# Four K matmuls held back behind the last modulation columns, and two quarters' modulation begun with 128 tokens

## Chip, cores, metric

One core of one Trainium2 chip. The metric is the device time of one execution in microseconds (us); lower is better. The verdict "faster" or "slower" needs 2%; what this study looks at is about 0.1%, so most of the evidence comes from profiles, in which times can be compared to a hundredth of a microsecond, and only the rest from the timed runs.

Names: PE is the tensor engine, PEld its weight loads, DVE the vector engine, ACT the scalar engine, POOL GpSimd, SP the engine that issues most transfers. PSUM is the memory that PE writes its results to, used by the kernel in eight banks. The span is the time from the first to the last instruction of a run. A transfer's slack is the time from its landing to the start of the instruction that needs it. L680 is line 680 of the kernel.

## The reference, cut to what matters

```python
x = A_x                                             # 1 x 2048 x 1024, bf16
mod = (silu(c) @ w_mod).reshape(1, 6, 1, -1)        # 6 x 1024 values
sa, ca, ga, sb, cb, gb = ...                        # its six rows
h = layernorm(x) * (1 + ca) + sa                    # <- the stretch studied here
x = x + ga * linear_attention(h, wqkv, wo)          # q, k, v = h @ wqkv; phi(k)^T v; ...
h = layernorm(x) * (1 + cb) + sb
x = x + gb * ((gelu(h @ w_gate) * (h @ w_up)) @ w_down)
```

The first matmuls on real data need `h`, and `h` needs `ca` and `sa`, which are themselves a matrix product of `silu(c)` with 4 MB of `w_mod`. The beginning of the kernel is therefore a pipeline of arrivals: x, `w_mod` in four quarters of 256 features each, and the K weights.

## The kernel before

Tokens come in chunks of 128; the first four chunks (0 to 3) share one tile of 512 tokens. The 1024 features are cut into eight slices `dc` of 128; quarter q of the modulation serves slices 2q and 2q+1. The parts that the change and the argument touch:

```python
def mods(Ht, rfn, sg, sc, s0, s1, dc0, dc1, tag):          # DVE: h = h * (1+ca) + sa, one slice at a time
    for dc in range(dc0, dc1):
        e.tensor_scalar(Ht[sg][:, dc, s0:s1], Ht[sg][:, dc, s0:s1], sA, sB, op0=mult, op1=add)
def mod1(c0, n, dc0, dc1): ...                              # the same, for n chunks from chunk c0

def mod_cols(q, bank):                                      # PE: 32 matmuls of one column each
    for t in range(2):                                      # t: ca or sa, each its own transfer of 512 KB
        for b in range(2):
            for dc in range(NDC):
                e.matmul(PS(bank, col, col + 1), WMQ[q][:, dc, t, b*P:(b+1)*P], SILUT[:, dc:dc+1], ...)
def mod_copy(q, bank): ...                                  # DVE: PSUM columns -> MODT, with the 1 of (1+ca)

# K of chunks 0 to 3: eight PSUM tiles of 128 tokens x 512 features, seven whole banks ...
kb0 = {(0,0): 0, (0,1): 1, (1,0): 2, (1,1): 3, (2,0): 5, (2,1): 6, (3,0): 7}
def k31(dcs, c0=0, c1=496): ...                             # ... and chunk 3's second half, 496 wide, in bank 4,
                                                            # whose last 16 columns hold the modulation columns
def k_part(q, cs):
    for dc in (2*q, 2*q + 1):
        for (c_, jg), b in kb0.items():
            if c_ in cs: kv_mm(c_, "k", jg, b, [dc])
        if 3 in cs: k31([dc])

# [...]
        k_part(0, [3])
        k_part(1, [3])
        mod_cols(2, 4)                 # third quarter's columns
        mod_copy(2, 4)
        warm(2)                        # two matmuls of zeros, no result
        mod1(0, 4, 4, 6)               # slices 4 and 5, all 512 tokens
        k_part(2, [0, 1, 2, 3])        # 16 K matmuls
        mod_cols(3, 4)                 # last quarter's columns
        mod_copy(3, 4)
        mod1(0, 4, 6, 8)               # slices 6 and 7
        for (c_, jg), b in kb0.items():
            kv_mm(c_, "k", jg, b, [6, 7])
        k31([6, 7])
        k31(list(range(NDC)), MC0, 512)   # the 16 columns left over
# [...] K is evacuated, then V, then everything else
```

## Time and profile before

| | before |
|---|---|
| time, median of 3 runs | 839.61 us (838.99 to 839.78) |
| span of the profiled execution | 836.77 us |
| first modulation columns start | 9.20 us |
| third quarter's columns start | 21.06 us |
| first V matmul starts | 31.57 us |

The page of the profile: span, busy time of the engines, and the chain of work that ended last.

```profile
span 836.8 us, 11359 instructions
...
PE 830.2 (99%) x4194; PEld 384.4 (46%) x4194; DVE 511.7 (61%) x895; ACT 336.1 (40%) x555; POOL 37.1 (4%) x91
...
PE 98%; DMA 1%; DVE 1%; SPq 0%; ACT 0%; issue 0%
```

PE is busy from end to end and the chain is 98% PE: the time is PE's stream of instructions plus its gaps. Which gaps there are is told by PE's waits in the whole run (engine, tile and line; what it waited for; us in total, times, longest).

```profile
PE ps_all L478 <- POOL bmask L429: 2.1, 1, 2.1
PE ps_all L680 <- DVE h1T L565: 1.3, 4, 0.7
PE ps_all L602 <- DMA wmq<-in_w_mod_dram: 0.6, 1, 0.6
```

Three lines, all in the first 30 us. The second is the one that the change is after: K matmuls (L680) that wait for the modulated h1T. They are seen in order of time in PE's timeline (start, us, engine, line, operation, what it writes and reads, shapes, count, and in brackets the idle time before it):

```profile
9.20 0.95 PE L602 MATMUL ps_all<-siluT,wmq 128*128 128x1 bf16 x32 [0.59 <-DMA wmq<-in_w_mod_dram]
...
21.06 0.94 PE L602 MATMUL ps_all<-siluT,wmq 128*128 128x1 bf16 x32
21.86 0.59 PE L736 MATMUL ps_all<-warm 128*128 128x512 bf16 x2
22.71 1.69 PE L680 MATMUL ps_all<-wk,h1T 128*128 128x512 bf16 x7 [0.25 <-DVE h1T L565]
24.23 0.37 PE L756 MATMUL ps_all<-wk,h1T 128*128 128x496 bf16 x1
24.44 1.67 PE L680 MATMUL ps_all<-wk,h1T 128*128 128x512 bf16 x7
25.95 0.37 PE L756 MATMUL ps_all<-wk,h1T 128*128 128x496 bf16 x1
26.16 0.94 PE L602 MATMUL ps_all<-siluT,wmq 128*128 128x1 bf16 x32
27.81 3.30 PE L680 MATMUL ps_all<-wk,h1T 128*128 128x512 bf16 x14 [0.71 <-DVE h1T L565]
30.95 0.77 PE L756 MATMUL ps_all<-wk,h1T 128*128 128x496 bf16 x10
31.57 0.81 PE L680 MATMUL ps_all<-wv,h1T 128*128 128x512 bf16 x3
```

And DVE's timeline of the same stretch:

```profile
22.04 0.16 DVE L611 TENSOR_TENSOR modt<-ps_all,add 128x4 f32<-128x4 f32 x1 [3.41 <-PE ps_all L602]
22.24 0.74 DVE L565 TENSOR_SCALAR h1T<-h1T,modt 128x512 bf16<-128x512 bf16 x2
27.14 0.16 DVE L611 TENSOR_TENSOR modt<-ps_all,add 128x4 f32<-128x4 f32 x1 [4.16 <-PE ps_all L602]
27.34 0.73 DVE L565 TENSOR_SCALAR h1T<-h1T,modt 128x512 bf16<-128x512 bf16 x2
```

The hand-over: last column matmul, copy by DVE, modulation of one slice by DVE, PE again. The 32nd column matmul starts at 26.94 and the next K matmul at 27.81, 0.87 us later. The same hand-over at 22 us is partly covered by the two matmuls of zeros (0.25 us of idle time before PE's restart instead of 0.71).

### The profile page before, as it was taken

The page shows a single profiled execution, that of the slowest core. Times are in us where ns is not written, and L with a number is a line of the kernel's source. Part 1 is how long each engine was busy: PE and PEld are TensorE (multiplying, and loading weights), DVE is VectorE, ACT ScalarE, POOL GpSimd, SP SyncE. Part 2 cuts the span into 40 slices and gives each one's busy share as a digit, 9 for nine tenths or more (in the row PEclk, how much of TensorE's full clock was granted, in tenths as well). Part 3 has the DMA queues.
Part 4 walks back from the last instruction along what each step waited for, and adds up shares of the span by engine and source line. Part 5 has one row for each costly group of instructions (what it writes and reads, how often), then busy time and mean ns, then how long its engine had stood idle before and what let it go on. Part 6 is the DMA issues. An engine that isn't in the chain of part 4 may idle for free.

```text
span 836.8 us, 11359 instructions
## 1 busy us (share of the span) xinstructions
PE 830.2 (99%) x4194; PEld 384.4 (46%) x4194; DVE 511.7 (61%) x895; ACT 336.1 (40%) x555; POOL 37.1 (4%) x91
## 2 busy tenths in 40 slices
PE   8999999999999999999999999999999999999998
PEld 4444444444444444444444444444444444444445
DVE  6678877687785577753455665356556535655512
ACT  2357777446423355420354442045554104445300
POOL 2012111000200000010000000000000000000000
DMA  9984422239696769180555533055553305555000
GB/s 291 312 251 101 102 76 76 78 79 235 140 236 204 224 202 277 28 194 26 158 151 151 152 101 76 19 158 152 151 151 101 76 20 159 152 154 145 7 19 26
DMA packets 184102, 113.22 MB, mean 135 GB/s; under 512 B 35560, under 2 KB 175080, under 8 KB 183024
## 3 DMA queue, kind: packets, MB, share of 16 engines
q1 hardware_dynamic: 184032, 112.50, 50.0%
q8 instruction: 33, 0.54, 0.3%
q14 instruction: 21, 0.17, 0.1%
q10 hardware_dynamic: 16, 0.00, 0.0%
HBM read 100.67 MB, written 4.47 MB: 126 GB/s over the span
## 4 chain that ended last, share of the span: by engine, by line
PE 98%; DMA 1%; DVE 1%; SPq 0%; ACT 0%; issue 0%
PE ps_all L1144 23%; PE ps_all L1116 23%; PE ps_all L1119 23%; PE ps_all L680 13%; PE ps_all L1059 7%; PE ps_all L721 7%; PE ps_all L702 1%; DMA wmq<-in_w_mod_dram 1%; PE ps_all L961 0%; PE ps_all L602 0%; DVE h1T L565 0%; PE ps_all L973 0%; PE ps_all L756 0%; PE ps_all L643 0%; SPq L442 0%; DVE st L742 0%
## 5 line engine op out<-in xcount | busy, mean ns | idle before, releaser
L1116 PE MATMUL ps_all<-h2T,wg 128*128 128x512 bf16 x896 | 339.6, 379 | 0.0
L1119 PE MATMUL ps_all<-h2T,wu 128*128 128x512 bf16 x896 | 339.6, 379 | 0.0
L1144 PE MATMUL ps_all<-wd,yT 128*128 128x512 bf16 (+3 forms) x952 | 194.2, 366 | 0.0
L1127 ACT ACTIVATE q<-ps_all 128x512 f32<-128x512 f32 x112 | 66.9, 597 | 225.3 <-PE ps_all L1116 221.5
L1144 PEld LDWEIGHTS ps_all<-wd,yT 128*128 128x128 bf16 x952 | 90.1, 98 | 103.9 <-issue 0.4
L1116 PEld LDWEIGHTS ps_all<-h2T,wg 128*128 128x128 bf16 x896 | 87.7, 98 | 105.8 <-issue 0.2
L1119 PEld LDWEIGHTS ps_all<-h2T,wu 128*128 128x128 bf16 x896 | 87.7, 98 | 105.7
L1132 DVE SCALAR_TENSOR_TENSOR ww<-th,guh 128x512 f32<-128x512 f32 x112 | 77.5, 692 | 77.9 <-ACT th L1131 77.9
L1129 DVE SCALAR_TENSOR_TENSOR ww<-q,ps_all 128x512 f32<-128x512 f32 x112 | 76.9, 686 | 77.7 <-ACT guh L1128 77.6
L1131 ACT ACTIVATE th<-ww 128x512 f32<-128x512 f32 x112 | 70.5, 629 | 87.3 <-DVE ww L1129 87.3
L1149 DVE TENSOR_TENSOR ps_all<-ps_all,gbb 128x512 f32<-128x512 f32 (+3 forms) x34 | 22.7, 667 | 94.8 <-PE ps_all L1144 94.8
L1134 DVE TENSOR_TENSOR yT<-ww,ps_all 128x512 bf16<-128x512 f32 x112 | 76.8, 686 | 3.8
L1128 ACT ACTIVATE guh<-ps_all 128x512 f32<-128x512 f32 x112 | 66.3, 592 | 0.0
L721 PE MATMUL ps_all<-h1T,wq 128*128 128x512 bf16 x256 | 58.7, 379 | 0.0
L680 PE MATMUL ps_all<-wk,h1T 128*128 128x512 bf16 x248 | 57.3, 379 | 1.3 <-DVE h1T L565 1.3
L669 ACT ACTIVATE eb<-ps_all 128x512 f32<-128x512 f32 x64 | 37.4, 600 | 50.6 <-PE ps_all L680 22.3
L680 PE MATMUL ps_all<-wv,h1T 128*128 128x512 bf16 x256 | 57.7, 379 | 0.0
L1059 PE MATMUL ps_all<-w,pq 128*128 128x512 bf16 x256 | 56.2, 379 | 0.0
L670 DVE TENSOR_SCALAR eb<-eb 128x512 f32<-128x512 f32 x64 | 27.1, 423 | 26.7 <-ACT eb L669 26.3
L1059 PEld LDWEIGHTS ps_all<-w,pq 128*128 128x128 bf16 x256 | 25.0, 98 | 30.2 <-issue 0.2
L680 PEld LDWEIGHTS ps_all<-wv,h1T 128*128 128x128 bf16 x256 | 24.9, 98 | 29.5
L680 PEld LDWEIGHTS ps_all<-wk,h1T 128*128 128x128 bf16 x248 | 23.8, 98 | 30.6 <-DVE h1T L565 3.1
(96 smaller groups left out, 481.0 us busy)
## 6 DMA issues: line engine op xcount, KB each, us to landing
wg<-in_B_w_gate_dram SPq DMA_DIRECT2D x56, 512.0 KB, 4.1
wu<-in_B_w_up_dram SPq DMA_DIRECT2D x56, 512.0 KB, 5.3
rb<-scr_rd SPq DMA_DIRECT2D x32, 256.0 KB, 6.6
wd<-in_B_w_down_dram SPq DMA_DIRECT2D x7, 1024.0 KB, 8.5
wmst<-in_w_mod_dram SPq DMA_DIRECT2D x6, 1024.0 KB, 6.8
wmq<-in_w_mod_dram SPq DMA_DIRECT2D x8, 512.0 KB, 7.7
out_dram<-xall SPq DMA_DIRECT2D x31, 128.0 KB, 1.7
xall<-in_A_x_dram SPq DMA_DIRECT2D x3, 1024.0 KB, 12.4
```

Of the source, the lines that this page charges most:

```text
L680: o = sch.op(T, lambda e, dc=dc: e.matmul(PS(bank), H1[sg][:, dc, ci * P:(ci + 1) * P], W_[:, dc, jg * 512:(jg + 1) * 512], start=(dc == 0 ...
L721: o = sch.op(T, lambda e, dc=dc: e.matmul(PS(b), WQ[:, dc, qc * P:(qc + 1) * P], H1[sg][:, dc, :], start=(dc == 0), stop=(dc == NDC - 1)), ...
L1059: last[half] = sch.op(T, lambda e, g=g, half=half: e.matmul(PS(b0 + half), PQ[sg][:, g, ci * P:(ci + 1) * P], W2[:, g, half * 512:(half + ...
L1116: og = sch.op(T, lambda e, dc=dc: e.matmul(PS(bg), WG[slot][:, dc, e_ * P:(e_ + 1) * P], H2[sg][:, dc, :], start=(dc == 0), stop=(dc == ND ...
L1119: ou = sch.op(T, lambda e, dc=dc: e.matmul(PS(bu), WU[slot][:, dc, e_ * P:(e_ + 1) * P], H2[sg][:, dc, :], start=(dc == 0), stop=(dc == ND ...
L1127: sch.op(A, lambda e: e.activation(Q1[j][:, :], PS(bg), ACTF.Square, scale=math.sqrt(GELU_A)), prd=pr(bg), wr=rq, note=f"q1 {fc}")
L1128: ogh = sch.op(A, lambda e: e.activation(GUH[j][:, :], PS(bg), ACTF.Copy, scale=0.5), prd=pr(bg), wr=rg, note=f"gh {fc}")
L1129: sch.op(V, lambda e: e.scalar_tensor_tensor(WW[j][:, :], Q1[j][:, :], 1.0, PS(bg), op0=ALU.add, op1=ALU.mult), rd=rq, prd=pr(bg), wr=rw, ...
L1131: sch.op(A, lambda e: e.activation(TH[j][:, :], WW[j][:, :], ACTF.Tanh, scale=GELU_C), rd=rw, wr=rt, note=f"th {fc}")
L1132: sch.op(V, lambda e: e.scalar_tensor_tensor(WW[j][:, :], TH[j][:, :], 1.0, GUH[j][:, :], op0=ALU.add, op1=ALU.mult), rd=rt + rg, wr=rw, n ...
L1134: sch.op(V, lambda e: e.tensor_tensor(YT[:, fc, :], WW[j][:, :], PS(bu), ALU.mult), rd=rw, prd=pr(bu), wr=r_yt(fc), note=f"yT {fc}")
L1144: o = sch.op(T, lambda e, b=b, fc=fc, c0=c0, c1=c1, n=n: e.matmul(PS(b, 0, n), YT[:, fc, ci * P:(ci + 1) * P], WDT[fc // 4][:, fc % 4, c0:c1],
```

## The change

The intent: fill the gap behind the last columns with K matmuls that need only slices already modulated, and shorten the hand-over by modulating the first 128 tokens of a slice, all that the first two matmuls need, in an instruction of their own.

```diff
         warm(2)
-        mod1(0, 4, 4, 6)
-        k_part(2, [0, 1, 2, 3])
+        mod1(0, 1, 4, 5)
+        mod1(1, 3, 4, 5)
+        mod1(0, 4, 5, 6)
+        k_part(2, [0, 1, 2])
         mod_cols(3, 4)
         mod_copy(3, 4)
-        mod1(0, 4, 6, 8)
+        mod1(0, 1, 6, 8)
+        mod1(1, 3, 6, 8)
+        for dc in (4, 5):
+            kv_mm(3, "k", 0, kb0[3, 0], [dc])
         for (c_, jg), b in kb0.items():
             kv_mm(c_, "k", jg, b, [6, 7])
-        k31([6, 7])
+        k31([4, 5, 6, 7])
```

The change was announced as six matmuls held back. The diff holds back four (chunk 3, two halves, slices 4 and 5): two go into the gap, and the two 496-wide ones go to the end of the block. Of the four modulations, three are split (slices 4, 6 and 7); slice 5 stays 512 wide.

## The prediction

> **What bounds the kernel.** The tensor engine (PE): 830.2 of 836.8 us busy (page part 1), the chain of waits is 98% PE. The wait list has three entries for PE in the whole run: 2.1 us at the start, 0.6 us for a w_mod transfer, 1.3 us in four waits for the modulated h1T. The change touches two or three of those four, all before 32 us.
>
> **The stretch, from the timeline.**
> - Third quarter: modulation columns copied at 22.04; the 128x512 modulation of slice 4 takes 0.412 us from 22.238; PE restarts at 22.71. 16 K matmuls follow, one per 0.216 us, to 26.16. [...]
> - Last columns: 32 one-column matmuls, 26.16 to 26.96. Copy at 27.14, slice 6 modulated from 27.338 (0.413 us), PE restarts at 27.81: 0.85 us without a PE start. The next matmul waits for slice 7 until 28.13, 0.10 us over the pitch.
>
> **What the change does.** No matmul is added or removed. By the diff I count four held back (chunk 3, both halves, slices 4 and 5), not six: two go into the gap behind the last columns, two to the end of the K block. Four modulations of 128x512 become four of 128x128 (0.306 us) and four of 128x384 (0.377 us).
>
> **Costs on the critical path.**
> 1. First modulation 128 wide: PE restarts 0.106 us earlier, near 22.60. The other 384 tokens are ready near 22.90; the third matmul starts at 23.05, so no new stall.
> 2. 12, not 16, matmuls before the columns: they begin near 25.20, end near 26.0. Their last wmq transfer landed at 25.31 by its semaphore and is needed near 25.4. This uses up almost all of the DMA's slack.
> 3. The gap: two matmuls (0.43 us) fill it. Copy near 26.18, slice 6 for the first 128 tokens ready near 26.74; PE still idles about 0.3 us.
> 4. Slice 7's 0.10 us stall disappears; the last wk slice landed at 26.59, needed near 26.97.
> 5. Two matmuls (0.42 us) follow at the end.
>
> Sum: 0.43 filled + 0.106 + 0.107 + 0.10 = about 0.74 us. The K block ends near 30.62, not 31.36. VectorE's evacuation begins about 1 us earlier, wv's first half landed at 28.95 and 30.35 (needed near 30.8 and 31.7), and PE has no wait afterwards: nothing should absorb the shift.
>
> **Prediction.** 838.9 us, 8 in 10 between 838.0 and 839.9, where the runs before spread from 838.99 to 839.78. Faster by over 2%: 0.003; within 2%: 0.994; slower by over 2%: 0.003.
>
> **What would show the steps.** PE's restart at 22.60; columns starting at 25.2 without a wait for wmq; two matmuls in the gap and 0.3 us idle; the first V matmul near 30.8, not 31.57; PE's waits on h1T falling from 1.3 to about 0.6 us; past 50 us the same pieces of the chain, all 0.7 us earlier.
>
> **What would make it wrong.** The last wmq transfer landing late: in this trace one of its 16 parts trails the others by about 1.4 us, and every delay past 25.4 now costs PE time one for one, where before there was 0.9 us of slack. The same for wk's last slice. Or a later transfer (x, wq, FFN weights) that takes the gain back, which I don't expect, as PE waits for none today.

## The result, and the profile after

The change is correct. Its median was 838.83 us (838.45 to 839.15, 6 runs), that of the kernel before 839.3 us (838.66 to 839.78, 6 runs). The ratio is 0.9994, 95% interval 0.9981 to 1.0007: same, by the 2% rule. The times alone can't tell 0.5 us from nothing.

The page of the profile after:

```profile
span 836.7 us, 11362 instructions
...
PE 830.1 (99%) x4194; PEld 384.4 (46%) x4194; DVE 512.2 (61%) x898; ACT 336.4 (40%) x555; POOL 37.4 (4%) x91
```

The spans differ by 0.03 us (836.77 and 836.74). A reader who stops here concludes that the change did nothing. PE's waits in the whole run say otherwise:

```profile
PE ps_all L478 <- DMA c<-in_c_dram: 2.4, 1, 2.4
PE ps_all L602 <- DMA wmq<-in_w_mod_dram: 1.1, 1, 1.1
PE ps_all L680 <- DVE h1T L565: 0.7, 4, 0.2
```

The wait for h1T fell from 1.3 to 0.7 us as intended, and the wait of the first columns for their transfer rose from 0.6 to 1.1 us. The change doesn't touch that transfer. PE's timeline:

```profile
9.85 0.95 PE L602 MATMUL ps_all<-siluT,wmq 128*128 128x1 bf16 x32 [1.08 <-DMA wmq<-in_w_mod_dram]
...
21.75 0.94 PE L602 MATMUL ps_all<-siluT,wmq 128*128 128x1 bf16 x32
22.55 0.59 PE L736 MATMUL ps_all<-warm 128*128 128x512 bf16 x2
23.30 2.76 PE L680 MATMUL ps_all<-wk,h1T 128*128 128x512 bf16 x12 [0.15 <-DVE h1T L565]
25.90 0.94 PE L602 MATMUL ps_all<-siluT,wmq 128*128 128x1 bf16 x32
26.70 0.59 PE L680 MATMUL ps_all<-wk,h1T 128*128 128x512 bf16 x2
27.45 3.20 PE L680 MATMUL ps_all<-wk,h1T 128*128 128x512 bf16 x14 [0.15 <-DVE h1T L565]
30.49 1.18 PE L756 MATMUL ps_all<-wk,h1T 128*128 128x496 bf16 x12
31.53 0.81 PE L680 MATMUL ps_all<-wv,h1T 128*128 128x512 bf16 x3
```

DVE's timeline of the same stretch (a row merges instructions of one line and shows the shape of the first):

```profile
22.73 0.16 DVE L611 TENSOR_TENSOR modt<-ps_all,add 128x4 f32<-128x4 f32 x1 [3.41 <-PE ps_all L602]
22.93 0.93 DVE L565 TENSOR_SCALAR h1T<-h1T,modt 128x128 bf16<-128x128 bf16 x3
26.88 0.16 DVE L611 TENSOR_TENSOR modt<-ps_all,add 128x4 f32<-128x4 f32 x1 [3.03 <-PE ps_all L602]
27.08 1.11 DVE L565 TENSOR_SCALAR h1T<-h1T,modt 128x128 bf16<-128x128 bf16 x4
```

Everything in this execution starts late: the first columns at 9.85 instead of 9.20, the third quarter's at 21.75 instead of 21.06. From there on it catches up. Measured from the start of the third quarter's columns to the first V matmul, which I call the stretch from here on, the kernel before takes 31.57 - 21.06 = 10.51 us and the changed one 31.53 - 21.75 = 9.78 us: 0.73 us less. From the first V matmul to the end both take 805.21 us (836.77 - 31.57 and 836.74 - 31.53). So the question became where the 0.65 us at the start comes from, whether it belongs to the change or to the execution, and whether the 0.73 us is real.

My theory: the stretch is a property of the kernel and the gain of 0.73 us reaches the end; the start of the first columns is a property of the execution, and PE carries it to the end in the same way. Rivals: the difference is scatter; one of the two halves of the change does all of it; something later takes it back.

### The profile page after: what moved, and what is told of

It is laid out like the page before. It is cut to its first block, busy times and chain, and to the rows that moved or that the text cites. A ratio compares the mean times of both kernels' runs of the same rounds, so it can differ in the third digit from the quotient of the medians.

```text
span 836.7 us, 11362 instructions
## 1 busy us (share of the span) xinstructions
PE 830.1 (99%) x4194; PEld 384.4 (46%) x4194; DVE 512.2 (61%) x898; ACT 336.4 (40%) x555; POOL 37.4 (4%) x91
## 2 busy tenths in 40 slices
DMA packets 184102, 113.22 MB, mean 135 GB/s; under 512 B 35560, under 2 KB 175080, under 8 KB 183024
## 3 DMA queue, kind: packets, MB, share of 16 engines
q1 hardware_dynamic: 184032, 112.50, 49.8%
## 4 chain that ended last, share of the span: by engine, by line
PE 98%; DMA 1%; DVE 0%; SPq 0%; ACT 0%; issue 0%
PE ps_all L1149 23%; PE ps_all L1121 23%; PE ps_all L1124 23%; PE ps_all L680 13%; PE ps_all L1064 7%; PE ps_all L721 7%; PE ps_all L702 1%; DMA wmq<-in_w_mod_dram 1%; PE ps_all L966 0%; PE ps_all L602 0%; PE ps_all L978 0%; PE ps_all L756 0%; PE ps_all L643 0%; SPq L442 0%; DVE h1T L565 0%; ACT h1T L548 0%
```

## The experiments

Eleven runs were made, of nine different kernels, all correct. Those of one group shared a chip and the runs of the kernel before. The table gives each profile: starts of the first (A), third (B) and last (C) quarter's columns and of the first V matmul (V), and the span, all in us. The last two columns are worked out from them.

| kernel | A | B | C | V | span | stretch V-B | span-A |
|---|---|---|---|---|---|---|---|
| before | 9.20 | 21.06 | 26.16 | 31.57 | 836.77 | 10.51 | 827.57 |
| before, again | 9.76 | 21.65 | 26.74 | 32.15 | 837.36 | 10.50 | 827.60 |
| change | 9.85 | 21.75 | 25.90 | 31.53 | 836.74 | 9.78 | 826.89 |
| change, again | 9.50 | 21.41 | 25.55 | 31.18 | 836.39 | 9.77 | 826.89 |
| change, third time | 9.60 | 21.47 | 25.62 | 31.25 | 836.46 | 9.78 | 826.86 |
| only held back | 9.85 | 21.72 | 25.97 | 31.80 | 837.02 | 10.08 | 827.17 |
| only split | 9.52 | 21.41 | 26.41 | 31.62 | 836.85 | 10.21 | 827.33 |
| four in the gap | 9.58 | 21.46 | 25.59 | 30.90 | 836.11 | 9.44 | 826.53 |
| eight held back | 9.36 | 21.21 | 24.50 | 31.46 | 836.68 | 10.25 | 827.32 |
| ten dummies | 9.32 | 21.21 | 25.36 | 32.81 | 838.03 | 11.60 | 828.71 |
| no warm-ups between | 9.93 | 20.95 | 25.19 | 30.49 | 835.72 | 9.55 | 825.79 |
| the same, again | 9.36 | 20.36 | 24.61 | 29.91 | 835.13 | 9.55 | 825.77 |
| x's chunk 3 first | 10.14 | 21.99 | 26.14 | 31.77 | 836.99 | 9.78 | 826.85 |

In all thirteen profiles the span less V is 805.21 or 805.22 us.

Two things bear on every time quoted below. First, the timed number is longer than the span, and not by the same amount for each kernel. The record lists both for most runs (the span to 0.1 us). Time less span was 1.75 to 1.85 us in all 36 such runs of the two kernels without the split (before, and only held back), and 2.10 to 2.22 us in all 52 runs of the kernels with it; the split adds three DVE instructions (898 for 895). So about 0.37 us of what these kernels gain inside the span is lost outside it. The two halves below isolate this to the split; where that time lies, and why, no run shows. Second, eight runs have a granted clock of 0.998 where all others listed have 1.000. They include every run over 840 us except those with the ten dummies.

### First group: the change and its halves

**The change again.**

> The changed kernel again, for a reference in the same rounds. The measure is the stretch from the first matmul of the third quarter's modulation columns to the first V matmul: 10.51 us in the profile of before, 9.78 us in that of the change. My theory: the stretch is again near 9.8 us whatever the start does, and the time is 0.5 to 0.9 us under before's, give or take the run scatter of about 0.4 us, which comes from where the first modulation columns start (9.20 us in before's profile, about 0.65 us later in that of the change). Rival 1, the 0.47 us between the medians is scatter alone: the difference falls on either side of zero. Rival 2, a later transfer takes the gain back: stretch 9.8 us, but the time from first V matmul to the end grows by 0.7 us.

Measured: stretch 9.77 us, first V matmul to the end 805.21 us. Time 838.59 us median (5 runs) against 839.17 us for before (9 runs): 0.58 us between the medians; ratio 0.9995, interval 0.9983 to 1.0008. The stretch repeats to 0.01 us, and rival 2 falls, since the rest of the span is not longer. The times alone still don't exclude rival 1. The spans of the same runs speak against it: their means are 836.58 and 837.34 us, 0.76 us apart, with only the ends of the two ranges touching (836.1 to 837.1, 837.0 to 838.0).

**Only the matmuls held back.**

```diff
-        mod1(0, 1, 4, 5)
-        mod1(1, 3, 4, 5)
-        mod1(0, 4, 5, 6)
+        mod1(0, 4, 4, 6)
...
-        mod1(0, 1, 6, 8)
-        mod1(1, 3, 6, 8)
+        mod1(0, 4, 6, 8)
```

> Only the four held-back matmuls, modulation 512 tokens wide as before. My theory counts 0.43 us for this half: stretch 10.51 - 0.43 = 10.08 us, two matmuls in the gap behind the last columns, idle rest about 0.4 us, time 0.43 us under before's. Rival (the split does all the work, holding back only shuffles matmuls): stretch 10.5 us.

Measured, with the two lines of PE's timeline that the stretch is read from:

```profile
21.72 0.94 PE L602 MATMUL ps_all<-siluT,wmq 128*128 128x1 bf16 x32
...
31.80 1.46 PE L680 MATMUL ps_all<-wv,h1T 128*128 128x512 bf16 x6
```

The stretch is 10.08 us, 0.43 us under before's, as expected. The second of the two held-back matmuls starts at 26.99 and the next at 27.62; less one matmul's 0.216 us that is 0.41 us idle. Time 838.73 us against 839.17 us. The rival, that holding back only shuffles matmuls, falls. Time less span is 1.81 us on average, as before's 1.80, so nothing of this half is lost outside the span.

**Only the split.** The kernel before, with the five `mod1` lines of the change and nothing else.

> Only the modulation begun with 128 tokens, no matmul held back. My theory counts 0.106 + 0.107 + 0.10 = 0.31 us: stretch 10.20 us, PE restarts 0.10 us earlier after each of the two copies, no slice-7 wait, no new wait for the other 384 tokens; time 0.3 us under before's. Rival (holding back does all): stretch 10.5 us. Rival 2 (the split stalls on the 384 tokens): stretch over 10.5 us.

Measured, by the same two lines:

```profile
21.41 0.94 PE L602 MATMUL ps_all<-siluT,wmq 128*128 128x1 bf16 x32
...
31.62 1.67 PE L680 MATMUL ps_all<-wv,h1T 128*128 128x512 bf16 x7
```

The stretch is 10.21 us, 0.30 us under before's. Time 839.0 us against 839.17 us. Here time less span is 2.17 us on average, against before's 1.80: the mean span, with the scatter of the start in it, is 0.46 us shorter than before's (836.88 and 837.34), the mean time only 0.09 us (839.05 and 839.14). So the gain of the split is real inside the span and is not shown in the timed number. The trace lacks some matmul records (11282 instructions, not 11362), among them the first of the 14 behind the columns, so I don't read the gap there from it; the later starts are not touched by that. Both rivals fall: the split gives its part and does not stall on the other 384 tokens. In the stretch the halves add up, 0.43 + 0.30 = 0.73 us, to what both together give.

**Four in the gap.** Between the starts at 26.92 and 27.45 the change leaves PE idle for 0.32 us. Its choice has a reason: the two 496-wide matmuls write bank 4, from which DVE reads the modulation columns in the gap. A first version of this experiment put them there, and the check for races ahead of a run refused it, because nothing orders that read and PE's writes to the same bank. It was never run, so what the chip would do is not shown. So the choice fell on other chunks, and chunk 2's second half serves:

```diff
-        k_part(2, [0, 1, 2])
+        for dc in (4, 5):
+            for (c_, jg), b in kb0.items():
+                if (c_, jg) not in ((2, 1), (3, 0)):
+                    kv_mm(c_, "k", jg, b, [dc])
+            k31([dc])
...
         for dc in (4, 5):
+            kv_mm(2, "k", 1, kb0[2, 1], [dc])
             kv_mm(3, "k", 0, kb0[3, 0], [dc])
...
-        k31([4, 5, 6, 7])
+        k31([6, 7])
```

> The change with another choice of the four: both slices of chunk 2's second half and of chunk 3's first half go into the gap, the two 496-wide ones stay ahead of the columns, none is left for the end. The columns start as in the change, so no more is asked of the DMA. My theory: the rest of the gap (about 0.3 us) is filled, stretch 9.78 - 0.3 = 9.45 to 9.5 us, no PE start gap over 0.25 us there, and the time about 0.3 us under the change's. Rival (the restart after the columns is set by something other than the modulation, the last wk slice for example): stretch stays at 9.8 us with PE idle again before slice 6 or 7.

Measured: PE's timeline has one unbroken run of K matmuls behind the columns, with no idle time of 0.1 us or more in it (one matmul record is missing in it):

```profile
25.59 0.94 PE L602 MATMUL ps_all<-siluT,wmq 128*128 128x1 bf16 x32
26.39 4.05 PE L680 MATMUL ps_all<-wk,h1T 128*128 128x512 bf16 x17
30.28 0.77 PE L756 MATMUL ps_all<-wk,h1T 128*128 128x496 bf16 x10
30.90 2.32 PE L680 MATMUL ps_all<-wv,h1T 128*128 128x512 bf16 x10
```

Stretch 9.44 us, 0.34 us under the change's; the rival falls. The times don't confirm it: 838.75 us median, because two of the five runs took 840.3 and 840.25 us (the others 838.1 to 838.75). Runs about 2 us longer than their neighbours occurred with other kernels too, before included (840.99, 841.01 and 841.41 us), all counted as fast because they are under 1.5% longer. Every one of them ran at a granted clock of 0.998 instead of 1.000; 0.2% of 836 us is, as an estimate, 1.7 us. What lowers the clock stays open, as none of them was profiled. The three runs here at 1.000 have a mean of 838.37 us, 0.39 us under the mean of the change's five (838.76), which fits the stretch but is no more than the scatter.

### Second group: the transfers, the end, one quarter earlier

**Eight held back.** This tests the warning of the prediction, that the last `w_mod` transfer has almost no slack left.

```diff
-        k_part(2, [0, 1, 2])
+        k_part(2, [0, 1])
...
-            kv_mm(c_, "k", jg, b, [6, 7])
+            kv_mm(c_, "k", jg, b, [4, 5, 6, 7] if c_ == 2 else [6, 7])
```

> The change with chunk 2's four matmuls of slices 4 and 5 held back too: 8 ahead of the last columns, two in the gap, six at the end. The columns then ask for their last wmq transfer 0.86 us earlier. My theory (its landing has almost no slack left): PE waits for wmq there, until just after the landing, unless the start was late as in the profile of the change (then part of the 0.86 us is slack); the wait is 0.1 to 0.9 us and the stretch grows from 9.8 by the same. Rival (the landing has room): no wait, stretch 9.8 us, time as the change's.

Measured: the columns break in two, at the point where the second of their two transfers is needed, in PE's timeline:

```profile
24.50 0.54 PE L602 MATMUL ps_all<-siluT,wmq 128*128 128x1 bf16 x16
25.36 0.55 PE L602 MATMUL ps_all<-siluT,wmq 128*128 128x1 bf16 x16 [0.32 <-DMA wmq<-in_w_mod_dram]
```

By its semaphore in the trace, that transfer's sixteenth and last part landed at 25.31; the 17th weight load starts at 25.36. The wait cost 0.484 us between starts where neighbours are 0.025 us apart, so 0.46 us, and the stretch is 10.25 - 9.78 = 0.47 us longer than the change's. Time 838.75 us against 838.81 us for before: no gain left to speak of in the time, although the stretch is still 0.26 us under before's. So there is a wall, and PE waited until just after the landing, as expected. The landing was at 25.31 here as in the first profile of before; over the thirteen profiles it came between 24.43 and 25.39. How close the change comes to it is another matter. The time from the landing to the 17th weight load was 0.55, 1.38 and 1.68 us in the three profiles of the change, and 1.23 and 2.58 us in the two of before. "Almost no slack" (0.1 us) was too dark for three reasons. It took 9.20 us, the earliest start of the thirteen, for the usual one; its profile held one of the three latest landings; and the 17th weight load comes 0.38 us after the columns' start where it doesn't wait, so from the predicted 25.20 it would have been needed at 25.58, not 25.4.

**Ten dummies.**

```diff
             kv_mm(3, "k", 0, kb0[3, 0], [dc])
+        warm(10)
```

> The change with ten matmuls of zeros put into the gap behind the last columns, after the two K matmuls: 10 x 0.2157 = 2.16 us less the 0.3 us of idle rest, so PE is 1.85 us late from there on. My theory (nothing after 32 us absorbs or multiplies a shift of PE): stretch 11.6 us, time 1.8 to 1.9 us over the change's. Rival (a later transfer or the other engines set the end): the time grows by clearly less than 1.8 us, and the first V matmul to the end is shorter than in the change.

Measured: the ten took 2.16 us in PE's timeline (from 26.59 to the next K matmul at 28.75), the pitch at which 16 K matmuls of before (two of them 496 wide) took 3.451 us (26.162 - 22.711 in the trace, 0.2157 us each). Stretch 11.60 us, 1.82 us over the change's; time 840.54 us (840.18 to 840.66), 1.73 us over before's 838.81 us on this chip, ratio 1.0017, interval 1.0004 to 1.0031. The change itself wasn't in this group. Against its 838.59 us of the other group, on another chip, the difference is 1.95 us, so that the 1.8 to 1.9 us expected of the time was not tested on one chip; the span less A is 1.82 us over the change's (828.71 and 826.89). From the first V matmul to the end the profile again shows 805.22 us. The rival falls: nothing in the span after the stretch absorbs a delay of PE.

**No warm-ups between.** Four in the gap, and the same one quarter earlier:

```diff
-        k_part(1, [0, 1, 2])
+        k_part(1, [0, 1])
+        kv_mm(2, "k", 0, kb0[2, 0], [2, 3])
...
-        k_part(1, [3])
+        k31([2, 3])
         mod_cols(2, 4)
         mod_copy(2, 4)
-        warm(2)
+        for dc in (2, 3):
+            kv_mm(2, "k", 1, kb0[2, 1], [dc])
+            kv_mm(3, "k", 0, kb0[3, 0], [dc])
```

> The same treatment one quarter earlier, on top of four in the gap: two matmuls of chunk 2 and two of chunk 3 (slices 2 and 3) behind the third quarter's columns in place of the two warm-up matmuls. PE's work before the last columns falls by 0.43 us of zeros and about 0.3 us of gap. My theory (the DMA is now the limit here): the columns wait for wmq transfers, third quarter's (landed 21.1 or 20.4) or last quarter's (25.3 or 24.6), and only a late start gains from it; the first V matmul comes about 5.4 to 5.6 us after the last wmq landing, and the time is 0 to 0.5 us under that of the four-in-gap kernel. Rival (PE limits here): no wait for wmq after the first columns, and 0.75 us under the four-in-gap kernel.

Measured: here my theory fell and the rival held. There was one wait for `w_mod` in PE's whole run, that of the first columns, and the span less A fell by the full 0.74 us below the four-in-gap kernel's (825.79 and 826.53). (The stretch, 9.55 us, is no fair measure here, as the columns it starts from come after fewer matmuls.) PE's timeline has no idle left behind either set of columns:

```profile
20.95 0.94 PE L602 MATMUL ps_all<-siluT,wmq 128*128 128x1 bf16 x32
21.75 2.10 PE L680 MATMUL ps_all<-wk,h1T 128*128 128x512 bf16 x9
...
25.19 0.94 PE L602 MATMUL ps_all<-siluT,wmq 128*128 128x1 bf16 x32
25.99 4.04 PE L680 MATMUL ps_all<-wk,h1T 128*128 128x512 bf16 x18
```

In this execution A came late, at 9.93, and the last transfer had landed at 24.43, 1.14 us before its weight load; the first V matmul came 6.06 us after that landing, not the 5.4 to 5.6 us of a kernel that waits for it. Time 837.87 us (837.44 to 838.94) against 838.81 us, ratio 0.9987, interval 0.9974 to 0.9999.

### Third group: the start, and the fastest kernel again

**The kernel before again**, for a second profile.

> The kernel before once more, for its profile: so far one profile stands for it. If the readings are properties of the kernel and not of one execution, the stretch is again 10.5 us, first V matmul to the end 805.2 us, and the span less the start of the first modulation columns 827.6 us, while that start itself may lie anywhere between 9.2 and 10 us.

Measured: 837.4 us of span, A at 9.76, stretch 10.50 us, span less A 827.60 us. As expected: the first profile of before had an early start, and nothing else differs. Against this profile the change's is 0.6 to 1.0 us shorter in span; against the first one, 0.03 to 0.4 us.

**x's chunk 3 first.** A cause was still missing for the scatter of A. It is always 0.04 to 0.05 us after the landing of one transfer (9.15 and 9.20 in before, 9.80 and 9.85 in the change), so delay that landing:

```diff
-        wmq_dma(0, (0,))
         x_dma(3, 4)
+        wmq_dma(0, (0,))
```

> The change with the 256 KB of x's chunk 3 sent ahead of the wmq transfer that the first modulation columns wait for. My theory (the run scatter of about half a microsecond enters where that transfer lands, and PE carries it to the end one for one): the columns start about 0.7 us later, at 10.2 to 10.6 us, the span less that start stays at 826.9 us, and the time is 0.5 to 0.7 us over the change's. Rival (VectorE or ScalarE set the pace there, not the landing): the columns start later, but the span less that start shrinks by about the same, and the time stays the change's.

Measured against the unmodified change on the same chip (next experiment). The first columns there, then here, in PE's timelines:

```profile
9.60 0.95 PE L602 MATMUL ps_all<-siluT,wmq 128*128 128x1 bf16 x32 [0.26 <-DMA wmq<-in_w_mod_dram]
```

```profile
10.14 0.95 PE L602 MATMUL ps_all<-siluT,wmq 128*128 128x1 bf16 x32 [1.50 <-DMA wmq<-in_w_mod_dram]
```

A came 0.54 us later, a little less than the 0.7 us that I expected, and the span grew by 0.53 us (836.46 to 836.99); span less A stayed (826.86 and 826.85). The rival, that DVE or ACT set the pace, falls. The medians differ by 0.29 us (839.15 and 838.86), but the other's contains two of the long runs; without these it is 0.53 us between the medians and 0.23 us between the means, so the times agree only roughly. So a late first landing costs its full delay at the end of the span, at least over this range.

**The change, third time.**

> The changed kernel beside the two others, on the same chip: stretch 9.78 us, span less the start of the first columns 826.9 us, first V matmul to the end 805.2 us; time 0.7 us under before's give or take 0.4.

Measured: stretch 9.78, span less A 826.86, V to the end 805.21 us. Time 838.86 us median (838.51 to 840.84, 6 runs, two of them over 840) against 839.55 us for before (838.78 to 841.41, 11 runs): 0.69 us between the medians; ratio 0.9998, interval 0.9984 to 1.0011. The two long runs, and two of before's, are the ones at a clock of 0.998; without them the means are 838.71 and 839.34 us, 0.63 us apart.

**No warm-ups between, again.**

> The fastest kernel so far (two quarters with four matmuls behind the columns, no warm-up matmuls between them) again, beside the changed kernel on the same chip: span less the start of the first columns 825.8 us if that start is late (9.8 us or more), up to 0.5 us more if it is early and the columns wait for their transfers; time 0.6 to 1.1 us under the change's. If it had been luck, the time is the change's.

Measured: A early this time, at 9.36, and still no wait for the later transfers; span less A 825.77 us. The last transfer landed 0.34 us before its weight load, so the 0.5 us that I allowed for an early start did not come. Time 837.39 us (837.06 to 838.39), 1.47 us under the change's median, which two long runs have raised (the profiles differ by 1.1 us in span less A), and 2.16 us under before's; ratio to before 0.9976, interval 0.9964 to 0.9988. By the 2% rule that is still "same", but this is the one version whose interval lies below 1, in both of its groups. Against the change on the same chip the means at a clock of 1.000 differ by 1.04 us (837.67 and 838.71), close to what the profiles say.

## Why the prediction was right, point by point

The predicted time, 838.9 us, lies 0.07 us from the measured 838.83, and 839.9 to 838.0 held it. That agreement is luckier than it looks: medians of before itself lay between 838.81 and 839.55 us on the three chips. Two errors also worked against each other in it. It subtracts 0.74 us from the median of the first three runs of before, 839.61, where that of six runs is 839.3; and it takes the whole sum to reach the timed number, where 0.37 us is lost outside the span and the medians came out 0.47 us apart. What deserves checking is the mechanism.

1. **First restart 0.106 us earlier: right, at 0.10 us.** From the third quarter's copy to PE's restart, 22.71 - 22.04 = 0.67 us before and 23.30 - 22.73 = 0.57 us after. The modulation took 0.412 us at 512 tokens and 0.314 us at 128. No stall on the other 384 tokens followed: the third K matmul starts 0.216 us after the second. In this pair of profiles the narrow first instruction came out ahead inside the span by 0.10 us at each of the two hand-overs (the second took 27.81 - 27.14 = 0.67 us before and 27.45 - 26.88 = 0.57 us after); DVE had been idle for 3.03 to 4.16 us there, and of its modulation only the first instruction was in the chain, 0.42 us before and 0.32 to 0.33 us after. (In the timed number the 0.37 us outside the span takes that back.) The prediction counted four pairs of split instructions; the diff makes three and leaves slice 5 whole, which changes nothing in the sum.
2. **Columns near 25.2, with almost no slack for their last transfer: the order was right, the size was wrong.** They start 4.14 to 4.15 us after the third quarter's columns, where before they took 5.10. (Predicted from before's 21.06: 4.14.) In absolute time they start at 25.55 to 25.90, and the slack was 0.55 to 1.68 us, not 0.1. One part is the start of everything: one profile's 9.20 us, for which the three profiles of the change have 9.50 to 9.85. The others are the late landing in that profile and the 0.38 us to the 17th weight load, as said under "Eight held back".
3. **Two matmuls in the gap, about 0.3 us idle left: right.** Second matmul at 26.92, next at 27.45, less 0.216: 0.32 us. Four in the gap removed it, which shows that it was idle time and not a limit.
4. **Slice 7's stall gone: right.** The distance of the second K matmul from the first behind the columns fell from 0.322 to 0.226 us.
5. **Two matmuls more at the end: right**, 0.42 us; the twelve instructions of L756 take 1.18 us for ten in 0.77 us.

The sum, predicted at 0.74 us, was 0.73 us in the stretch, and 0.71 us in span less A (827.57 and 827.60 against 826.86 to 826.89), and nothing inside the span absorbed it: 805.21 us from V to the end in both. What the prediction did not have is the 0.37 us outside the span: in the timed number about half of the sum remains, and "nothing should absorb the shift" is right for the span only. The prediction's pitch of 0.216 us for 512 columns held in the profiles of before and of the change: the 32 K and V matmuls that stand in the chain at 50.35 and 50.32 us take 6.91 us in both, 0.216 us each.

One test that the prediction set itself failed in its letter: "past 50 us the same pieces of the chain, all 0.7 us earlier". In the two profiles at hand they are 0.04 us earlier; the first full block of Q matmuls in the chain of waits stands, before and then after, at

```profile
46.90 3.45 PE ps_all L721 x16
```

```profile
46.86 3.45 PE ps_all L721 x16
```

So do the other absolute marks it named (22.60, 25.2, 30.8). They were tied to an execution, not to an event that both kernels share. Compared from a common event, each one fits.

## What to carry to other kernels

When an engine that is the bottleneck waits for a short hand-over to another engine and back, hold back just as much work that is already ready as the gap is long, and make the first instruction of the hand-over only as large as its first consumer needs; the two gains add up, as 0.43 + 0.30 us did here in the span. Then compare the span with the timed number run by run: here the second measure cost 0.37 us outside the span, more than it gained inside. Before you compare two profiles by their spans, anchor both on an event that both kernels share: here a scatter of 0.7 us at the first landing hid a gain of 0.73 us in one pair and would have shown 1.0 us in another. And count a transfer's slack over several executions: it was 0.55 to 1.68 us for one kernel, and only holding back twice as much ran into it.

## What else the traces show

- The parts of one transfer did not land together in these two profiles. All the large transfers went through one queue ("hardware_dynamic" in the profile, 112.50 of 113.22 MB in both first profiles), and parts trailed all the same: of the last `wmq` transfer of before, fifteen of sixteen parts had landed by 23.85 us and the last one at 25.31; in the first profile of the change fourteen by 23.87, the last two at 24.35 and 24.60. The semaphore's counts don't say which DMA engines moved them, so that stays open.
- The bf16 modulation of one slice (L565) in the first profiles of before and the change: one instruction lasts 306 to 316 ns for 128 columns and 406 to 413 ns for 512. Where another follows at once, it starts 222 to 230 ns after one of 128 and 328 ns after one of 512. By starts, the 384 further columns cost 101 ns (328 less the median 227).
- With the same order of transfers the first columns' start moved between 9.20 and 9.93 us over twelve profiles, and it came out one for one in the span: the span less that start stayed at 826.86 to 826.89 us over the three profiles of the change. The executions some 2 us longer than the rest, in which no profile was taken, all have a granted clock of 0.998; what lowers it is not explained by anything here.
- The part of the timed number outside the span differed between kernels this alike: 1.75 to 1.85 us without the three further DVE instructions of the split, 2.10 to 2.22 us with them.
